# Causal masks of one more attention batch on TensorE, whole-tile copies of its scores, and a new first place in the ring of weight tiles

## The chip, the cores and the metric

One core of one Trainium2 chip. The time is in device microseconds (us) for one execution of the whole program. Engines go by the profile's names: PE is TensorE (PEld its weight loads), DVE is VectorE, ACT is ScalarE, POOL is GpSimd, SP is SyncE, which here issues the DMAs. PE, DVE and ACT each run their own list of instructions in the order in which the program has them.

## What is computed

Four batches of causal attention with a memory read-out (8 heads, 576 positions, 64 wide), then two gated layers on all 2304 tokens (512 wide, 1536 hidden):

```
scores = q k^T / 8, masked where key > query;  a = softmax(scores);  local = a v
mem    = phi(q) M_prev / (phi(q) z_prev);       x = g mem + (1 - g) local
xn     = x / rms(x) * rms_g
y      = (silu(xn w_gate) * (xn w_val)) w_out            # first layer
out    = (sigmoid(y w_gate2) * (y w_val2)) w_out2        # second layer
```

The weights come as float64.

## The kernel before

**Groups.** Tokens are worked through in five groups, numbered by `g`. Group -1 holds the first 128 positions of all four batches; groups 0 to 3 hold positions 128 to 575 (448 tokens) of one batch each, the *long* groups. For each group the main loop runs both layers (`l` = 0, 1), each over 12 slices `f` of 128 hidden units. One slice is 12 matmuls for the gate (tile `pg`), 12 for the value (`pv`), some work of ACT and DVE that makes the hidden tile `h` of them, and 12 matmuls (`po`) that add the slice's share of the output; `po` of slice f stands behind `pg` and `pv` of slice f+1. While group g is in its layers, the attention of batch g+1 is worked through in small steps (`att_steps`) between the slices, so the attention of long batch 0 lies inside group -1, and that of batch 1 inside group 0.

**Attention of a head.** `att_scores` makes transposed scores in four PSUM tiles (`ps1` to `ps4`, two buffers), with keys on the partitions. They leave PSUM for the tile `sc`; then DVE takes maxima (`mx`), POOL the maximum over partitions (`mb`), DVE subtracts it, ACT takes the exponential and writes its fp16 upper half, DVE the lower half (`pt`). `att_av` multiplies with v (`pav`), `att_mem` reads the memory (`pm`) for two heads at a time.

**The mask.** In batch 0, `st_mm` adds it inside PSUM by one more 128x128 bf16 matmul a diagonal block (`tri_b` or `tri4_b` times `ident_b`), four a head, and ACT copies each head's scores in eight pieces. In batches 1 to 3 the four diagonal blocks are written to `sc` by DVE, which adds the mask (`tri`) on the way, and the other four pieces by ACT.

**The hand-over.** After its last head, a batch is normalised (`att_norm`): ACT squares (`junk`), a row of small DVE operations for the inverse root, then for each of four tiles of 128 tokens `att_xT` has DVE scale (`xn`), ACT write the upper fp16 half and DVE the lower one (both into `x`), and SP issue a DMA transpose into `ha`. Every `pg` matmul of the next group's first slice reads columns of all four tiles, so it waits for the last transpose.

**Weights.** `slot` deals out weight tiles in a ring by the counter `ring["w"]`: in group -1 over 7 tiles (`ws`, `wl`), from group 0 on over 13, the six tiles `wr` and `wrl` being the buffers that held raw float64 weights (`raw`, `rawl`) up to then. In group 0 a gate/value pair is loaded as float32 (`both`), scaled and split into fp16 by ACT, POOL and DVE (`halve`: line 674 sums, 676 maximum, 680 upper half, 681 lower half); a slice takes three tiles there.

**Order.** The program is written step by step, and a scheduler with a model of time then sets each engine's order; `issue_after` keeps some steps behind marks of earlier slices.

Of the kernel before, what the change touches and what calls it, by code (L numbers as in the profile page):

```python
# [25 lines left out]
SO = (0, 448, 896, 1216, 1408)  # L26
SW = 1536

NEARLY = 4
NLATE = 3  # L30
# [26 lines left out]
def attn_moe_moe_kernel(ctx, tc, qT, kT, qk0, v, mz, beta, w8, rms_g, outT):  # L57
# [6 lines left out]
    nc = tc.nc  # L64
# [24 lines left out]
        out=tri, in_=tri, compare_op=ALU.is_ge, fill=NEG, base=0, pattern=[[1, 128]], channel_multiplier=-1  # L89
# [7 lines left out]
    tri_b = const.tile([128, 128], BF16, name="tri_b")  # L97
    nc.scalar.copy(out=tri_b, in_=tri)
    tri4_b = const.tile([128, 128], BF16, name="tri4_b")
# [96 lines left out]
    def softmax_weights(sc, n):  # L196
        nc.scalar.activation(out=sc[:, 0:n], in_=sc[:, 0:n], func=AF.Exp, scale=scale)  # L197
        pt = ap_.tile([128, 2, SW], F16, tag="pt", name="pt")
        nc.scalar.copy(out=pt[:, 0, 0:n], in_=sc[:, 0:n])  # L199
        nc.vector.tensor_tensor(out=pt[:, 1, 0:n], in0=sc[:, 0:n], in1=pt[:, 0, 0:n], op=ALU.subtract)  # L200
        return pt

    def st_mm(ps, c0, kq, k0, q0, n, mask=None):
        kk, qq, q2 = kq
        for i, r in enumerate((qq, q2)):
            nc.tensor.matmul(  # L206
                ps[:, c0:c0 + n], kk[:, k0:k0 + 128], r[:, q0:q0 + n], start=(i == 0), stop=(i == 1 and not mask)
            )
        if mask:
            nc.tensor.matmul(ps[:, mask[0]:mask[0] + 128], ident_b, mask[1], start=False, stop=True)  # L210
# [247 lines left out]
    def att_scores(g, h):  # L458
        kq = st.pop(("qk", g, h))
        sc = ap_.tile([128, SW], F32, tag="sc", bufs=2, name="sc")  # L460

        def diag(ps, c, kt):
            d = SO[kt]
            if g == 0:
                nc.scalar.copy(out=sc[:, d:d + 128], in_=ps[:, c:c + 128])
                return
            nc.vector.tensor_tensor(  # L467
                out=sc[:, d:d + 128], in0=ps[:, c:c + 128], in1=(tri4 if kt == 4 else tri), op=ALU.add
            )

        def cp(ps, c, d, n):
            nc.scalar.copy(out=sc[:, d:d + n], in_=ps[:, c:c + n])  # L472

        ps = late["ps"].tile([128, 512], F32, tag="pa", name="ps1")
        st_mm(ps, 0, kq, 0, 128, 448)
        cp(ps, 0, 0, 448)
        ps = late["ps"].tile([128, 512], F32, tag="pa", name="ps2")
        st_mm(ps, 0, kq, 128, 128, 448, (0, tri_b) if g == 0 else None)
        diag(ps, 0, 1)
        cp(ps, 128, SO[1] + 128, 320)  # L480
        ps = late["ps"].tile([128, 512], F32, tag="pa", name="ps3")
        st_mm(ps, 0, kq, 256, 256, 320, (0, tri_b) if g == 0 else None)
        st_mm(ps, 320, kq, 384, 384, 192, (320, tri_b) if g == 0 else None)
        diag(ps, 0, 2)
        cp(ps, 128, SO[2] + 128, 192)
        diag(ps, 320, 3)
        cp(ps, 448, SO[3] + 128, 64)
        ps = late["ps"].tile([128, 512], F32, tag="pa", name="ps4")
        st_mm(ps, 0, kq, 448, 384, 192, (64, tri4_b) if g == 0 else None)
        diag(ps, 64, 4)  # L490

        mx = ap_.tile([128, 512], F32, tag="mx", bufs=1, name="mx")
        nc.vector.tensor_tensor(out=mx[:, 0:448], in0=sc[:, 0:448], in1=sc[:, 448:896], op=ALU.max)
        for kt in (2, 3, 4):
            q = SQ[kt] - 128
            nc.vector.tensor_tensor(  # L496
                out=mx[:, q:448], in0=mx[:, q:448], in1=sc[:, SO[kt]:SO[kt] + 448 - q], op=ALU.max
            )
        mb = ap_.tile([128, 512], F32, tag="mb", bufs=1, name="mb")
        nc.gpsimd.partition_all_reduce(mb[:, 0:448], mx[:, 0:448], channels=128, reduce_op=bass_isa.ReduceOp.max)  # L500
        nc.vector.tensor_tensor(
            out=sc[:, 0:896].rearrange("p (k q) -> p k q", k=2),
            in0=sc[:, 0:896].rearrange("p (k q) -> p k q", k=2),
            in1=mb[:, None, 0:448].to_broadcast([128, 2, 448]),
            op=ALU.subtract,
        )
        for kt in (2, 3, 4):
            q, d = SQ[kt] - 128, SO[kt]
            nc.vector.tensor_tensor(  # L509
                out=sc[:, d:d + 448 - q], in0=sc[:, d:d + 448 - q], in1=mb[:, q:448], op=ALU.subtract  # L510
            )
        st["pt", g, h] = softmax_weights(sc, SW)
# [104 lines left out]
    ring = {"w": 0, "top": 0, "raw": 0}  # L617
# [46 lines left out]
    def is_half(g, l, f):  # L664
        return g >= 0 and (l == 0 or f >= NWIDE)
# [317 lines left out]
    def last_of(e):  # L983
        return next(i for i in reversed(nc.cur_bb.bb.instructions) if i.engine == e)

    def behind(pairs):

        stack = ExitStack()
        for pair in pairs:
            for i in pair:  # L990
                stack.enter_context(tc.issue_after(i))
        return stack

    for g in range(-1, B):
        n = 512 if g < 0 else S - 128
        steps = list(att_steps(g + 1)) if g + 1 < B else []

        total = 2 * NF - (6 if g < 0 else 4)

        wait = 2 if g == 0 else 1  # L1000
        done, used = 0, 0
        for l in range(2):
            early = 2 if g < 0 and l == 0 else 0
            ws, hs = early_ws[:early], early_hs[:early]
            for f in range(early):
                hidden(ws[f], l, f, 256, g, xt, hs[f], 256)
            po = None
            for f in range(NF + 1):
                if f < NF:
                    if f >= early:  # L1010
                        if g > 0 and l == 1 and f == NWIDE:
                            mid = NF if g < B - 1 else NF // 2 + 2
                            for e, c in ((nc.vector, slice(NWIDE, mid)), (nc.gpsimd, slice(mid, NF))):
                                if c.start < c.stop:
                                    e.tensor_scalar(
                                        out=unit[2][:, c],
                                        in0=unit[1][:, c],
                                        scalar1=st["half_is1"],
                                        scalar2=None,
                                        op0=ALU.mult,  # L1020
                                    )
                        with behind(marks[-2:-1] if g == 0 else []):
                            ws.append(weights(g, l, f))
                        hs.append(htiles(g, l, f))
                        hidden(ws[f], l, f, n, g, xh if l == 1 and is_half(g, l, f) else xt, hs[f])
                        marks.append(tuple(last_of(e) for e in (mybir.EngineType.Activation, mybir.EngineType.DVE)))
                if f > 0:
                    if po is None:
                        po = [late[f"po{d // 2}"].tile([128, NMAX], F32, tag=f"po{d}", name="po") for d in range(KD)]
                    out_share(ws[f - 1], hs[f - 1], po, f - 1, n)  # L1030
                    done += 1
                    with ExitStack() as after:

                        if g < 0 and done < 5:
                            traced = nc.cur_bb.bb.instructions
                            for e in (mybir.EngineType.Activation, mybir.EngineType.DVE, mybir.EngineType.SP):
                                after.enter_context(
                                    tc.issue_after(next(i for i in reversed(traced) if i.engine == e))
                                )
                        while used < len(steps) and used < len(steps) * (done - wait) // (total - wait):  # L1040
                            with behind(marks[-2:-1] if g >= 0 else []):
                                steps[used]()
                            used += 1
            if g < 0 and l == 0:
                begin.close()
            xn = wide_tokens("cd") if l == 0 else None
            for d in range(KD):
                evacuate(l, d, n, g, po[d], xn)
            if l == 0 and g >= 0:
                xh = half_tokens("b")  # L1050
                halve_tokens(n, po, xh)
            if l == 0 and g < 0:
                token_scale()
            xt = xn
        xt = st.pop("xt", None)
# [55 lines left out]
```

## Time and profile before

| | |
|---|---|
| median of 3 runs | 1062.34 us (1061.07 to 1064.21) |
| the profiled execution | 1061.58 us |
| its span, first to last instruction | 1059.8 us |
| PE busy (share of the span) | 1036.0 us (98%) |
| DVE busy | 732.3 us (69%) |
| ACT busy | 550.7 us (52%) |
| POOL busy | 90.8 us (9%) |

The span is what the views of the trace cover; 1.8 us of the execution's time lie around it. Busy shares are means over the whole span and differ much between its parts. A PE row's duration includes the pipeline's latency, so rows that follow each other overlap, and what a matmul takes of PE is read from the starts.

### The profile page before, as it was taken

What the parts mean: (1) busy time and instruction counts of PE and PEld (TensorE: products, weight loads), DVE (VectorE), ACT (ScalarE), POOL (GpSimd) and SP (SyncE); (2) the same over time, 40 slices, a digit from 0 to 9 for tenths busy, and PEclk for the clock granted to TensorE, in tenths of its full rate; (3) what the DMA queues carried; (4) which work ended last, traced back from release to release, by engine and by line L of the source; (5) the groups of instructions that cost most, each with busy time, mean ns of one, the idle gap of its engine ahead of it and who ended that gap; (6) DMA issues with size and microseconds to landing.
All of it is one profiled execution on the core that took longest, in us unless ns stands there. A gap on an engine that the chain in (4) does not pass through costs nothing.

```text
span 1059.8 us, 17506 instructions
## 1 busy us (share of the span) xinstructions
PE 1036.0 (98%) x6445; PEld 749.7 (71%) x6445; DVE 732.3 (69%) x1588; ACT 550.7 (52%) x1074; POOL 90.8 (9%) x85
## 2 busy tenths in 40 slices
PE   8899999999999989999999999999999999999998
PEld 5778887888666757676667867766777766667665
DVE  5969999898669989865677866638788654224111
ACT  4668877775568757864454543425455432112111
POOL 2301012000001101110010110000101000000000
PEclk8999999999999999999999999999999999999999
DMA  6499998884885764589754453675455437445410
GB/s 267 149 353 377 322 358 286 305 277 154 251 310 200 241 221 159 183 282 309 239 174 159 170 184 128 171 260 186 154 177 173 147 120 222 145 148 172 173 45 36
DMA packets 89686, 222.15 MB, mean 210 GB/s; under 512 B 23808, under 2 KB 29952, under 8 KB 89472
## 3 DMA queue, kind: packets, MB, share of 16 engines
q1 hardware_dynamic: 89600, 221.03, 61.7%
q8 instruction: 51, 0.84, 0.3%
q14 instruction: 35, 0.29, 0.1%
HBM read 173.28 MB, written 44.04 MB: 205 GB/s over the span
## 4 chain that ended last, share of the span: by engine, by line
PE 85%; DVE 6%; ACT 4%; DMA 2%; issue 2%; SPq 0%; ACTq 0%; DVEq 0%
PE pg L792 25%; PE po L845 25%; PE pv L792 24%; PE ps L206 4%; PE pm L565 1%; PE pav L516 1%; PE pav L518 1%; PE pav L517 1%; DMA g_bc<-in_rms_g 1%; ACT sc L197 1%; PE po L842 1%; DMA out_T<-o 1%; DMA wl<-kept 0%; DVE x L609 0%; DMA ha<-x 0%
## 5 line engine op out<-in xcount | busy, mean ns | idle before, releaser
L809 ACT ACTIVATE t<-pg,unit 128x448 f32<-128x448 f32 x88 | 55.6, 632 | 138.0 <-PE pg L792 138.0
L845 PE MATMUL po<-h,ws 128*128 128x448 f32 (+1 forms) x504 | 121.9, 384 | 0.7 <-ACT h L824 0.7
L792 PEld LDWEIGHTS <-ws 128*128 128x128 f16 x672 | 63.1, 99 | 62.6 <-issue 9.3
L845 PEld LDWEIGHTS po<-h,ws 128*128 128x128 f32 x504 | 93.8, 188 | 13.6 <-ACT h L824 0.8
L845 PE MATMUL po<-h,wl 128*128 128x448 f32 (+1 forms) x396 | 95.5, 384 | 0.0
L792 PEld LDWEIGHTS <-wr 128*128 128x128 f16 x600 | 55.8, 98 | 53.7 <-issue 5.6
L500 POOL PARTITION_ALL_REDUCE mb<-mx x32 | 59.3, 1853 | 376.9 <-DVE mx L496 360.6
L824 ACT CAST h<-t 128x448 fp32r<-128x448 f32 (+1 forms) x70 | 40.6, 581 | 87.5 <-DVE t L813 79.9
L819 DVE SCALAR_TENSOR_TENSOR t<-t,pv 128x448 f32<-128x448 f32 (+1 forms) x60 | 37.8, 630 | 68.6 <-PE pv L792 65.0
L845 PE MATMUL po<-h,wr 128*128 128x448 f32 x348 | 81.0, 377 | 0.6 <-DVE h L829 0.5
L811 DVE SCALAR_TENSOR_TENSOR t<-t,pg 128x448 f32<-128x448 f32 (+2 forms) x60 | 37.2, 619 | 64.0 <-ACT t L809 64.0
L792 PEld LDWEIGHTS <-wl 128*128 128x128 f16 x504 | 47.4, 99 | 48.1 <-issue 6.2
L845 PEld LDWEIGHTS po<-h,wl 128*128 128x128 f32 x396 | 73.8, 188 | 9.8
L845 PEld LDWEIGHTS po<-h,wr 128*128 128x128 f32 x348 | 64.9, 188 | 7.7 <-DVE h L829 0.9
L472 ACT COPY sc<-ps 128x448 f32<-128x448 f32 (+3 forms) x128 | 46.9, 372 | 42.7 <-DVE sc L467 29.7
L197 ACT ACTIVATE sc<-sc 128x1536 f32<-128x1536 f32 x32 | 47.5, 1485 | 35.2 <-DVE sc L509 35.0
L200 DVE TENSOR_TENSOR pt<-sc,pt 128x1536 f16<-128x1536 f32 x32 | 56.1, 1752 | 6.2 <-ACT pt L199 6.1
L206 PE MATMUL ps<-qq,kk 128*128 128x448 f32 (+2 forms) x160 | 55.6, 352 | 3.0 <-ACT sc L472 3.0
L825 DVE TENSOR_TENSOR h<-t,h 128x448 fp32r<-128x448 f32 (+1 forms) x70 | 46.2, 660 | 16.8 <-ACT h L824 16.3
L828 ACT ACTIVATE h<-t,unit 128x448 fp32r<-128x448 f32 x40 | 26.7, 667 | 52.3 <-DVE t L819 52.1
L792 PEld LDWEIGHTS <-wrl 128*128 128x128 f16 x336 | 31.3, 98 | 30.2 <-issue 2.5
L813 DVE SCALAR_TENSOR_TENSOR t<-t,kappa,pv 128x448 f32<-128x448 f32 x48 | 32.5, 678 | 26.1 <-PE pv L792 25.1
(259 smaller groups left out, 2474.5 us busy)
## 6 DMA issues: line engine op xcount, KB each, us to landing
raw<-in_w SPq DMA_DIRECT2D x50, 511.8 KB, 6.3
wr<-parts SPq DMA_DIRECT2D x33, 512.0 KB, 3.5
ws<-parts SPq DMA_DIRECT2D x32, 512.0 KB, 3.4
kept<-w SPq DMA_DIRECT2D x48, 256.0 KB, 5.2
wl<-parts SPq DMA_DIRECT2D x24, 512.0 KB, 3.8
ws<-half SPq DMA_DIRECT2D x23, 512.0 KB, 3.2
rawl<-in_w SPq DMA_DIRECT2D x22, 511.8 KB, 6.4
kd<-in_kT SPq DMA_DIRECT2D x64, 144.0 KB, 3.8
```

What stands on the lines that cost most here:

```text
L197: nc.scalar.activation(out=sc[:, 0:n], in_=sc[:, 0:n], func=AF.Exp, scale=scale)
L200: nc.vector.tensor_tensor(out=pt[:, 1, 0:n], in0=sc[:, 0:n], in1=pt[:, 0, 0:n], op=ALU.subtract)
L206: nc.tensor.matmul(ps[:, c0:c0 + n], kk[:, k0:k0 + 128], r[:, q0:q0 + n], start=(i == 0), stop=(i == 1 and not mask))
L472: nc.scalar.copy(out=sc[:, d:d + n], in_=ps[:, c:c + n])
L500: nc.gpsimd.partition_all_reduce(mb[:, 0:448], mx[:, 0:448], channels=128, reduce_op=bass_isa.ReduceOp.max)
L792: nc.tensor.matmul(ps[:, 0:n], w[:, a, k * 128:(k + 1) * 128], x[b][:, k, o:o + n], start=(i == 0), stop=(i == 3 * KD - 1))
L809: nc.scalar.activation(out=t, in_=pg[:, 0:n], func=AF.Tanh, scale=u[:, 0:1] if half else 0.5)
L811: nc.vector.scalar_tensor_tensor(out=t, in0=t, scalar=1.0, in1=pg[:, 0:n], op0=ALU.add, op1=ALU.mult)
L819: nc.vector.scalar_tensor_tensor(out=t, in0=t, scalar=1.0, in1=pv[:, 0:n], op0=ALU.add, op1=ALU.mult)
L824: nc.scalar.copy(out=hi, in_=t)
L825: nc.vector.tensor_tensor(out=lo, in0=t, in1=hi.bitcast(F32), op=ALU.subtract)
L845: nc.tensor.matmul(po[d][:, 0:n], w[2][:, a, c], hh[:, b, 0:n], start=(f == 0 and i == 0), stop=(f == NF - 1 and i == 2))
```

## The change

Three things. In `att_scores` the flag `by_pe` is true for batches 0 and 1 (before, batch 0 alone had the mask on PE), so batch 1's masks go from DVE to 32 more PE matmuls (4 a head, 8 heads). Where PE masks, the scores leave PSUM in four whole ACT copies of 448, 448, 512 and 128 columns, in place of eight pieces (batch 0) or of four pieces by ACT and four by DVE (batch 1). And at group 0 the ring's counter is set to 7, so that the first weight tiles of that group are those that held float64 weights, and every later tile's place in the ring moves by two.

```diff
+        by_pe = g <= 1
+
         def diag(ps, c, kt):
             d = SO[kt]
-            if g == 0:
-                nc.scalar.copy(out=sc[:, d:d + 128], in_=ps[:, c:c + 128])
-                return
             nc.vector.tensor_tensor(
                 out=sc[:, d:d + 128], in0=ps[:, c:c + 128], in1=(tri4 if kt == 4 else tri), op=ALU.add
             )
...
+        def mask(c, m):
+            return (c, m) if by_pe else None
...
-        st_mm(ps, 0, kq, 128, 128, 448, (0, tri_b) if g == 0 else None)
-        diag(ps, 0, 1)
-        cp(ps, 128, SO[1] + 128, 320)
+        st_mm(ps, 0, kq, 128, 128, 448, mask(0, tri_b))
+        if by_pe:
+            cp(ps, 0, SO[1], 448)
+        else:
+            diag(ps, 0, 1)
+            cp(ps, 128, SO[1] + 128, 320)
...
-        diag(ps, 0, 2)
-        cp(ps, 128, SO[2] + 128, 192)
-        diag(ps, 320, 3)
-        cp(ps, 448, SO[3] + 128, 64)
+        if by_pe:
+            cp(ps, 0, SO[2], 512)
+        else:
+            diag(ps, 0, 2)
+            cp(ps, 128, SO[2] + 128, 192)
+            diag(ps, 320, 3)
+            cp(ps, 448, SO[3] + 128, 64)
...
-        st_mm(ps, 0, kq, 448, 384, 192, (64, tri4_b) if g == 0 else None)
-        diag(ps, 64, 4)
+        st_mm(ps, 0, kq, 448, 384, 192, mask(64, tri4_b))
+        if by_pe:
+            cp(ps, 64, SO[4], 128)
+        else:
+            diag(ps, 64, 4)
...
         wait = 2 if g == 0 else 1
+        if g == 0:
+            ring["w"] = NEARLY + NLATE
```

The scheduler orders the engines anew. Lines of the changed kernel from `att_scores` on stand 11 further down (804 of before is 815 there), so `pv` is line 792 before and 803 now, `pm` 565 and 576.

**PE, end of group -1.** Before, at the last memory read-out of batch 0 (`pm`), which stands inside the value matmuls of slice 9:

```order
L518 MATMUL pav<-vh_119,pt 128x65
L565 MATMUL pm<-mzt,ph 128x130 x2
L792 MATMUL pv<-xc,wl 128x512
L792 MATMUL pv<-xd,wl 128x512
L792 MATMUL pv<-xc,wl 128x512
L845 MATMUL po<-h,wl 128x512 x12
L792 MATMUL pg<-xc,ws 128x512
```

Now, at the same read-out, which stands between gate and value of slice 10:

```order
L576 MATMUL pm<-mzt,ph 128x130 x2
L803 MATMUL pv<-xc,ws 128x512
L803 MATMUL pv<-xd,ws 128x512
L803 MATMUL pv<-xc,ws 128x512 x2
L803 MATMUL pv<-xd,ws 128x512
L803 MATMUL pv<-xc,ws 128x512 x2
L803 MATMUL pv<-xd,ws 128x512
L803 MATMUL pv<-xc,ws 128x512 x2
L803 MATMUL pv<-xd,ws 128x512
L803 MATMUL pv<-xc,ws 128x512
L856 MATMUL po<-h,ws 128x512 x12
L803 MATMUL pg<-xc,wl 128x512
```

Up to the first `pg` of group 0 there stood 99 more matmuls of layers behind it (3 `pv`, then `po`, `pg`, `pv`, `po`, `pg`, `pv`, `po`, `po` of 12 each); now there stand 72 (`pv`, `po`, `pg`, `pv`, `po`, `po`).

**DVE, the same end of group -1.** Before, from the end of the inverse root (587) to slice 11: scaling (604), lower halves (609), the lower half of `h` (825), products with `pv` (819; the second is slice 11's), weight splits (623):

```order
L587 SCALAR_TENSOR_TENSOR ri<-nr,ri 128x4
L604 SCALAR_TENSOR_TENSOR xn<-x,ri,g_bc 128x512 x2
L819 SCALAR_TENSOR_TENSOR t<-t,pv 128x512
L609 TENSOR_TENSOR x<-xn,x 128x512 x2
L604 SCALAR_TENSOR_TENSOR xn<-x,ri,g_bc 128x512
L825 TENSOR_TENSOR h<-t,h 128x512
L604 SCALAR_TENSOR_TENSOR xn<-x,ri,g_bc 128x512
L623 TENSOR_TENSOR wr<-w,wr 128x512
L609 TENSOR_TENSOR x<-xn,x 128x512 x2
L819 SCALAR_TENSOR_TENSOR t<-t,pv 128x512
```

Now, in part (598 is the inverse root's last, 615 scales, 620 makes lower halves, 692 is `halve`'s split, 830 is slice 11's product, 903 an output copy):

```order
L598 SCALAR_TENSOR_TENSOR ri<-nr,ri 128x4
L615 SCALAR_TENSOR_TENSOR xn<-x,ri,g_bc 128x512 x2
L692 SCALAR_TENSOR_TENSOR wr<-wr,s_3346 128x512 x2
L620 TENSOR_TENSOR x<-xn,x 128x512 x2
L830 SCALAR_TENSOR_TENSOR t<-t,pv 128x512
L615 SCALAR_TENSOR_TENSOR xn<-x,ri,g_bc 128x512 x2
L836 TENSOR_TENSOR h<-t,h 128x512
L653 TENSOR_SCALAR pw<-wtop 128x2
L634 TENSOR_TENSOR wrl<-w,wrl 128x512
L655 TENSOR_SCALAR inv<-pw 128x2
L620 TENSOR_TENSOR x<-xn,x 128x512
L903 TENSOR_SCALAR o<-po 128x512
```

All four lower halves stood ahead of slice 11's product with `pv`; now two stand behind it (the last one two rows below the piece shown, behind an output copy). The splits of group 0's first weights (692), which stood behind all of this, now stand among it.

**DVE, end of group 0.** Before, from the inverse root's last operation (829 is the lower half of `h`; the product 819 is slice 11's):

```order
L587 SCALAR_TENSOR_TENSOR ri<-nr,ri 128x4
L604 SCALAR_TENSOR_TENSOR xn<-x,ri,g_bc 128x512 x2
L829 SCALAR_TENSOR_TENSOR h<-t,unit_124,h 128x448
L609 TENSOR_TENSOR x<-xn,x 128x512 x2
L604 SCALAR_TENSOR_TENSOR xn<-x,ri,g_bc 128x512 x2
L609 TENSOR_TENSOR x<-xn,x 128x512 x2
L819 SCALAR_TENSOR_TENSOR t<-t,pv 128x448
```

Now the same stretch:

```order
L598 SCALAR_TENSOR_TENSOR ri<-nr,ri 128x4
L615 SCALAR_TENSOR_TENSOR xn<-x,ri,g_bc 128x512 x2
L830 SCALAR_TENSOR_TENSOR t<-t,pv 128x448
L620 TENSOR_TENSOR x<-xn,x 128x512 x2
L615 SCALAR_TENSOR_TENSOR xn<-x,ri,g_bc 128x512
L840 SCALAR_TENSOR_TENSOR h<-t,unit_124,h 128x448
L615 SCALAR_TENSOR_TENSOR xn<-x,ri,g_bc 128x512
L620 TENSOR_TENSOR x<-xn,x 128x512
L903 TENSOR_SCALAR o<-po 128x448
L620 TENSOR_TENSOR x<-xn,x 128x512
```

Slice 11's product moved from behind the four lower halves to ahead of them. On PE the last read-out of batch 1 stood one `pv` matmul before the end of slice 9 and now stands seven before the end of slice 10.

## Rows read from the trace of the kernel before

**Rows 1.** The page, part 1: busy us (share) xinstructions.

```profile
PE 1036.0 (98%) x6445; PEld 749.7 (71%) x6445; DVE 732.3 (69%) x1588; ACT 550.7 (52%) x1074; POOL 90.8 (9%) x85
```

**Rows 2.** Stretches: length, busy PE, PEld, DVE, ACT, POOL, granted clock, DMA, GB/s.

```profile
287.30:291.90 4.60, 4.49 (x14) 1.75 (x15) 2.83 (x4) 2.38 (x6) 0.00 (x0) 0.63 1.03 340
...
320.00:420.00 100.00, 94.57 (x658) 69.52 (x657) 92.55 (x217) 72.03 (x151) 14.07 (x15) 0.98 0.58 198
494.40:587.00 92.60, 92.59 (x595) 63.65 (x596) 64.24 (x134) 39.63 (x67) 7.03 (x5) 1.00 0.61 204
```

**Rows 3.** Chain of waits: start us, us, what; first gates of groups 1, 2.

```profile
494.41 2.43 PE pg L792 x12
...
689.22 2.43 PE pg L792 x12
```

**Rows 4.** Timeline of PE, end of group -1: start, us, line, [idle before <-releaser].

```profile
261.72 0.69 PE L565 MATMUL pm<-mzt,ph 128*128 128x130 f32 x4
...
271.18 2.96 PE L845 MATMUL po<-h,ws 128*128 128x512 f32 x12
273.98 0.40 PE L792 MATMUL pg<-xc,wl 128*128 128x512 f32 x1
...
282.40 2.89 PE L845 MATMUL po<-h,wl 128*128 128x512 f32 x12
287.35 0.55 PE L792 MATMUL pg<-ha,wl 128*128 128x448 f16 x2 [2.05 <-ACT wl L680]
```

**Rows 5.** Line 612, the transposes: windows 278 to 300, then 470 to 500.

```profile
DMA to landing us min/median/max: 3.5/4.3/5.0
...
DMA to landing us min/median/max: 2.7/3.9/4.9
```

**Rows 6.** DVE by form, 262 to 279: busy us, mean ns | idle before.

```profile
L604 DVE SCALAR_TENSOR_TENSOR xn<-x,ri,g_bc 128x512 f32<-128x512 f32 x4 | 2.9, 747 | 0.0
L609 DVE TENSOR_TENSOR x<-xn,x 128x512 f16<-128x512 f32 x4 | 2.6, 684 | 0.0
...
L586 DVE TENSOR_TENSOR nr<-nr,ss 128x4 f32<-128x4 f32 x3 | 0.5, 162 | 0.1
```

**Rows 7.** Waits of PE, 300 to 412: us in total, times, longest.

```profile
PE ps L206 <- ACT sc L472: 2.3, 2, 1.6
```

**Rows 8.** Timeline of PE in group 0, first layer.

```profile
376.92 4.11 PE L792 MATMUL pg<-ha,ws 128*128 128x448 f16 x12 [0.46 <-DVE t L811]
```

**Rows 9.** Timeline of PE: scores with a mask (batch 0), without (batch 1).

```profile
105.19 0.23 PE L210 MATMUL ps<-tri_b,ident_b 128*128 128x128 bf16 x1
105.23 0.34 PE L206 MATMUL ps<-qq,kk 128*128 128x192 f32 x1
...
105.52 0.23 PE L210 MATMUL ps<-tri_b,ident_b 128*128 128x128 bf16 x1
...
338.73 0.25 PE L206 MATMUL ps<-qq,kk 128*128 128x192 f32 x1
...
338.93 0.28 PE L206 MATMUL ps<-qq,kk 128*128 128x192 f32 x1
```

**Rows 10.** Line 467, DVE's masks: ns min/median/max, first and last start.

```profile
L467 DVE TENSOR_TENSOR sc<-ps,tri x96: 273/284/294, 317.7 to 851.4; 128x128 f32<-128x128 f32 x96
```

**Rows 11.** ACT by form, 300 to 480: copies of scores.

```profile
L472 ACT COPY sc<-ps 128x448 f32<-128x448 f32 x8 | 4.2, 524 | 5.8 <-PE ps L206 5.8
L472 ACT COPY sc<-ps 128x320 f32<-128x320 f32 x8 | 3.3, 414 | 1.4 <-DVE sc L467 1.4
```

**Rows 12.** Waits of PE, 158 to 176, group -1: us in total, times, longest.

```profile
PE pg L792 <- ACT t L809: 1.1, 1, 1.1
```

**Rows 13.** Timeline of PE, end of group 0.

```profile
477.84 2.44 PE L792 MATMUL pg<-hb,wr 128*128 128x448 f16 x12
...
484.83 2.44 PE L792 MATMUL pg<-hb,wr 128*128 128x448 f16 x12
...
491.79 2.60 PE L845 MATMUL po<-h,wrl 128*128 128x448 f32 x12
```

More of the change, by code (lines that the diff above doesn't have):

```diff
@@ L477, in att_scores @@
         ps = late["ps"].tile([128, 512], F32, tag="pa", name="ps2")
-        st_mm(ps, 0, kq, 128, 128, 448, (0, tri_b) if g == 0 else None)
-        diag(ps, 0, 1)
-        cp(ps, 128, SO[1] + 128, 320)
-        ps = late["ps"].tile([128, 512], F32, tag="pa", name="ps3")
-        st_mm(ps, 0, kq, 256, 256, 320, (0, tri_b) if g == 0 else None)
-        st_mm(ps, 320, kq, 384, 384, 192, (320, tri_b) if g == 0 else None)
-        diag(ps, 0, 2)
-        cp(ps, 128, SO[2] + 128, 192)
-        diag(ps, 320, 3)
-        cp(ps, 448, SO[3] + 128, 64)
-        ps = late["ps"].tile([128, 512], F32, tag="pa", name="ps4")
-        st_mm(ps, 0, kq, 448, 384, 192, (64, tri4_b) if g == 0 else None)
-        diag(ps, 64, 4)
+        st_mm(ps, 0, kq, 128, 128, 448, mask(0, tri_b))
[4 more added lines that the diff above has]
+            cp(ps, 128, SO[1] + 128, 320)
+        ps = late["ps"].tile([128, 512], F32, tag="pa", name="ps3")
+        st_mm(ps, 0, kq, 256, 256, 320, mask(0, tri_b))
+        st_mm(ps, 320, kq, 384, 384, 192, mask(320, tri_b))
+        if by_pe:
[5 more added lines that the diff above has]
+            cp(ps, 448, SO[3] + 128, 64)
+        ps = late["ps"].tile([128, 512], F32, tag="pa", name="ps4")
+        st_mm(ps, 0, kq, 448, 384, 192, mask(64, tri4_b))
[3 more added lines that the diff above has]
+            diag(ps, 64, 4)
         mx = ap_.tile([128, 512], F32, tag="mx", bufs=1, name="mx")
```

## The prediction

> **What bounds the kernel now.** I read the page's busy shares first: PE is busy 98% of the span [rows 1], so what the change moves matters only where PE stands still, runs at its lower clock, or gets more to do. So next the starts of each group's first gate. Group 0 starts at 287.35 [rows 4], group 1 at 494.41 and group 2 at 689.22 [rows 3]: group 0 takes 207.1 us and group 1 takes 194.8, with the same matmuls. These 12.3 us are what a change to group 0 can win there. The stretches say what they are: from 320 to 420 PE has 5.4 us idle while DVE is busy 92.6 of 100, whereas group 1's first layer has PE without a gap and DVE at 64 of 92.6 [rows 2]. PE's waits in that part of group 0 are short and of many kinds, the largest for scores that leave PSUM [rows 7]. After one of them twelve gates took 4.11 us [rows 8] where they otherwise take 2.43 [rows 3]: the granted clock had dropped to its half, and that costs 1.7 us each time. One more such place is the hand-over from group -1 to 0: the last `po` ends at 285.29, PE stands 2.05 us for the upper half of the first weights (line 680) [rows 4], and the next 4.6 us have a mean clock of 0.63 [rows 2].
>
> **The masks on PE.** With a mask, a block of scores of 192 columns takes 0.33 us from one mask matmul's start to the next (105.19 to 105.52); without, 0.20 (338.73 to 338.93) [rows 9]. The mask's own slot is only 0.04 us (105.19 to 105.23), the rest is the weight load of the next matmul, which so short a matmul doesn't cover. So 0.13 us, times 32 in group 0: **+4.2 us**, all of it on PE, the engine that bounds. Bounds: 32 x 0.04 = 1.3 (if all the loads hide) and 32 x 0.23, the whole duration of a mask row, = 7.4. The Trainium skill, in "TensorE: Matmul & The Clock Gate", section "Back-to-back issue gap", gives about 81 ns per matmul of 128 columns in a stream of loads and matmuls. By that the masks would cost 2.6 us and the sum would end 1.6 us lower. The rows here are above it, since the neighbours of these masks are float32r with longer loads, and I go by the rows.
>
> **What DVE and ACT get.** DVE loses 32 masks of 0.28 us [rows 10], 9 us at most, most of it where it is near full. ACT's count of copies in batch 1 stays at four a head but 512 columns more go through them; 128 columns cost 0.11 us (524 against 414 ns) [rows 11], so 0.44 us a head, 3.5 us in all, under cover of an ACT that is busy 72 of 100 us [rows 2]; without that cover it would stand on the path of the scores, +3.5. In batch 0 ACT saves four copies a head; PE has next to nothing to gain from that in group -1, save one wait of 1.1 us for a `tanh` [rows 12] behind an exponential, which stands ahead of that exponential in the new order: **-1.1** (bounds -1.8, with a smaller wait for scores beside it, and 0). In group 0 the scores no longer pass between DVE and ACT in turns. Of the 7.1 us (5.4 idle, 1.7 of half clock) I take two thirds as gone: **-5**. The bounds are 0 (DVE is still some 86 of 100, and other waits are behind the first) and 12.3 less the half clock at the group's start, -10.5.
>
> **Weight tiles.** The first weights of group 0 now load while slices 10 and 11 of group -1 run, and ACT's work on them lies ahead of the `po` that end it. So the wait of 2.05 us for line 680 goes. What is late next is the input, `ha`.
>
> **Hand-over to group 0.** The new order has batch 0's last read-out (`pm`) later: 72 matmuls stand behind it in place of 99. Twelve take 2.80 us (271.18 to 273.98) [rows 4], so PE reaches the first gate 6 x 2.8 = 16.8 us after it; before it was 285.29 less 262.41 = 22.9. In that time the normalisation must finish, and its last pieces are in DVE's queue behind other work. From slice 10's product with `pv` (which cannot start before that `pv` ends, 2.8 + 0.3 for the latency = 3.1 us) to the last lower half, DVE's list has 17 instructions of 512 columns and 18 of a few columns. The long ones take 0.65 us each in a row (2.6 us for four of line 609, a little more for 604), the short ones 0.2 (0.162 and a third of the 0.1 idle before three of them) [rows 6]: 17 x 0.65 + 18 x 0.2 = 14.6, ending at 17.7 without any wait. The last transpose is issued then and lands 3.5 us later at the soonest of this hand-over [rows 5], at 21.2. PE waits 4.4 us as a floor, and I take 4.8, with some waiting on ACT and POOL in that chain; in place of 2.05 that is **+2.8** (bounds +1.5 with a landing of 2.7, the shortest seen, and +4). The half clock after it is there before and after. Nothing else can run: all of group 0 stands behind this gate in PE's list.
>
> **Hand-over to group 1.** The same happens at the end of group 0. Before, the gates start at 494.41 [rows 3], 2.62 us after the last twelve `po` started [rows 13]: no gap. Now `pm` has behind it 7 `pv` (1.3 us), `po` (2.4), the whole of a slice (477.84 to 484.83, 7.0) and the last `po` (2.6) [rows 13]: 13.3 us. Slice 11's `pv` ends at 8.2. Its product on DVE, from 8.5 on, has behind it eight long instructions up to the last lower half, where before all lower halves were ahead of it: 9 x 0.63 = 5.7, so 14.2; with a landing of 2.7 to 3.9 [rows 5] `ha` is there at 16.9 to 18.1. PE waits 3.6 to 4.8 us where it waited for nothing: **+4.2**. Such a gap was followed by half clock above, so **+1.7** more. Later hand-overs keep their order.
>
> **The sum:** 4.2 - 1.1 - 5 + 2.8 + 4.2 + 1.7 = +6.8. The profiled execution took 1061.58 us, so 1068.4. The median of the three runs is 0.8 above that execution, so against it the same working gives 1069; I say 1068.5.
>
> **Rivals.**
> 1. *Both inputs arrive in time* (ends on the other side). For it: before, they did at all hand-overs. Against: the counts above. It decides at one point, whether the last transpose lands before the last `po` ends, for which DVE's stretch would have to be over 4 us shorter in both places. Then the old gap and its half clock go too: 4.2 - 1.1 - 5 - 2.05 - 1.7 = -5.7, so 1056; with all of group 0's loss gone, 1050.
> 2. *DVE still bounds group 0.* The stalls there only change their names: for it, DVE's 92.6 of 100 loses no more than a tenth, and the 5.4 us were of many kinds. Then +11.8, 1073.4.
> 3. *No change.* Group 0 loses all of its stalls (-10.5) and the hand-overs cost their floors (2.3 and 3.6): 4.2 - 1.1 - 10.5 + 2.3 + 3.6 + 1.7 = +0.2, so 1061.8. For it: with DVE at 64 of 92.6, group 1 has no stall at all.
>
> **Chances.** The forecast 0.5, rival 1 0.09, rival 2 0.2, rival 3 0.21. A measurement here tells about 0.3% (3.2 us) from no change. Faster by more than that (under 1059.2) is rival 1, with a little of rival 3: 0.1. Within it (up to 1065.5): rival 3 and the forecast's lower end, 0.24. Slower: 0.66. The forecast's own range is 1064 to 1072; for 8 in 10 it reaches over rivals 2 and 3: 1058 to 1075.
>
> **What would show it.** Right: at both hand-overs PE's first gate waits 3 to 6 us for `ha` from the DMA, each followed by a mean clock near 0.6; the wait for line 680 is gone; 32 mask matmuls in group 0 with 0.3 us from mask to mask within a tile; DVE's line of masks at 64; PE idle from 320 to 420 under 3 us. Wrong: gates that start with the end of the last `po` at either hand-over (rival 1), or idle of 5 us and more in group 0's first layer (rival 2), or under 1 us there (rival 3). I am wrong also if the new places of tiles in the ring make weights late in groups 1 to 3, which the sum has at nothing: there the pairs are loaded several slices ahead, and a late one would cost a PE wait of a microsecond or two each.

## The result, and the profile after

The changed kernel takes 1067.26 us (median of 5 runs, 1065.77 to 1069.02) where the kernel before takes 1062.34: a ratio of 1.0052, interval 1.0039 to 1.0064. It is slower by half a per cent, 1.2 us less than forecast. The profiled execution took 1067.58 us, 6.0 more than that of before; the working had +6.8.

The page of the changed kernel, part 1, answers to [rows 1]: PE has 32 instructions more, DVE 32 fewer, and PE's share falls by a point, since the span has grown by more than PE's work.

```profile
PE 1038.0 (97%) x6477; PEld 750.9 (70%) x6477; DVE 728.9 (68%) x1556; ACT 552.5 (52%) x1042; POOL 90.1 (8%) x85
```

PE's timeline at the first gates of groups 0, 1 and 2 (start, us, line, idle before it and what ended it):

```profile
289.02 3.81 PE L803 MATMUL pg<-ha,wr 128*128 128x448 f16 x12 [4.20 <-DMA ha<-x]
...
497.69 4.63 PE L803 MATMUL pg<-ha,ws 128*128 128x448 f16 x12 [6.96 <-DMA ha<-x]
...
695.38 2.43 PE L803 MATMUL pg<-ha,wrl 128*128 128x448 f16 x12 [0.26 <-DMA ha<-x]
```

The reader is to see two things: what stands in the brackets, and the time of twelve gates behind it. At groups 0 and 1 PE now waits for the input, 4.20 and 6.96 us; before it was 2.05 for weights [rows 4] and nothing [rows 3, 13]. Twelve gates take 2.43 us at full clock and 4.63 behind the longer wait. The stretches say the same (columns as in [rows 2]): the start of group 0, its first layer, the gap ahead of group 1, and the start of group 1.

```profile
289.00:293.60 4.60, 4.58 (x17) 2.07 (x18) 0.76 (x2) 1.23 (x2) 0.00 (x0) 0.69 0.97 290
320.00:420.00 100.00, 98.86 (x673) 72.34 (x672) 88.63 (x196) 77.57 (x161) 13.28 (x15) 1.00 0.63 216
...
490.70:497.70 7.00, 0.04 (x2) 0.04 (x2) 0.65 (x1) 0.54 (x1) 0.00 (x0) 0.68 1.10 222
...
497.70:502.30 4.60, 4.60 (x13) 1.86 (x14) 0.62 (x1) 0.00 (x0) 0.00 (x0) 0.50 0.92 273
```

From 320 to 420 PE's idle time fell from 5.4 to 1.1 us, and DVE from 92.6 to 88.6 of 100. PE's waits from 300 to 412 were of five kinds, the largest of them in [rows 7]; one is left:

```profile
PE pav L529 <- DVE pt L200: 1.0, 1, 1.0
```

So the change does in group 0 what it says, and pays for it at two gates. The chain of waits ahead of group 1's gate (start, us, what) shows which work the gate waited for:

```profile
484.39 1.24 DVE xn L615 x2
485.73 0.62 DVE t L830
486.34 1.20 DVE x L620 x2
487.54 0.66 DVE xn L615
488.21 0.61 DVE h L840
...
490.65 0.70 DVE x L620
491.36 1.33 SPq L623
492.78 4.78 DMA ha<-x
497.69 4.63 PE pg L803 x12
```

It is read from below: the gate waits for a transpose under way for 4.78 us; this one stood on SP's queue (SPq) behind the transpose ahead of it; and that behind the normalisation on DVE, among which slice 11's product (830) and hidden tile (840) stand.

### The profile page after: what moved, and what is told of

It reads as the page before. It is cut to its first block, busy times and chain, and to the rows that moved or that the text cites. A ratio compares the mean times of both kernels' runs of the same rounds, so it can differ in the third digit from the quotient of the medians.

```text
span 1065.8 us, 17489 instructions
## 1 busy us (share of the span) xinstructions
PE 1038.0 (97%) x6477; PEld 750.9 (70%) x6477; DVE 728.9 (68%) x1556; ACT 552.5 (52%) x1042; POOL 90.1 (8%) x85
## 4 chain that ended last, share of the span: by engine, by line
PE 87%; ACT 3%; DVE 2%; DMA 2%; issue 1%; SPq 0%; ACTq 0%; POOL 0%; DVEq 0%; POOLq 0%
PE pg L803 26%; PE po L856 26%; PE pv L803 25%; PE ps L206 4%; PE pm L576 1%; PE pav L527 1%; PE pav L529 1%; PE pav L528 1%; DMA ha<-x 1%; PE po L853 1%; DMA ws<-parts 1%; PE ps L210 0%; ACT t L820 0%; ACT pt L199 0%; ACT vh L169 0%
## 5 line engine op out<-in xcount | busy, mean ns | idle before, releaser
L856 PE MATMUL po<-h,ws 128*128 128x448 f32 (+1 forms) x480 | 117.3, 385 | 0.2
L803 PEld LDWEIGHTS <-wr 128*128 128x128 f16 x624 | 58.4, 99 | 60.2 <-issue 6.3
L856 PEld LDWEIGHTS po<-h,ws 128*128 128x128 f32 x480 | 89.1, 188 | 13.1 <-ACT h L835 0.5
L856 PE MATMUL po<-h,wr 128*128 128x448 f32 x372 | 85.9, 376 | 0.0
L856 PEld LDWEIGHTS po<-h,wr 128*128 128x128 f32 x372 | 69.8, 188 | 6.8
L471 ACT COPY sc<-ps 128x448 f32<-128x448 f32 (+5 forms) x128 | 52.4, 421 | 41.3 <-DVE sc L466 23.0
L206 PE MATMUL ps<-q,kk 128*128 128x448 f32 (+2 forms) x160 | 49.4, 318 | 0.0
```

The costliest lines, as they stand in the source:

```text
L206: nc.tensor.matmul(ps[:, c0:c0 + n], kk[:, k0:k0 + 128], r[:, q0:q0 + n], start=(i == 0), stop=(i == 1 and not mask))
L803: nc.tensor.matmul(ps[:, 0:n], w[:, a, k * 128:(k + 1) * 128], x[b][:, k, o:o + n], start=(i == 0), stop=(i == 3 * KD - 1))
L856: nc.tensor.matmul(po[d][:, 0:n], w[2][:, a, c], hh[:, b, 0:n], start=(f == 0 and i == 0), stop=(f == NF - 1 and i == 2))
```

## The terms, measured

| term | forecast | measured | from |
|---|---|---|---|
| 32 masks on PE | +4.2 | +3.3 | starts on PE in group 0: 21 masks stand ahead of a float32r matmul and take 0.04 us, and that matmul 0.085 more; 11 stand ahead of a 16-bit one and take 0.055 to 0.067 |
| `tanh` wait, group -1 | -1.1 | -0.9 | this wait: 1.1 before, 0.2 now (the group as a whole ended 0.5 sooner, 284.82 for 285.29) |
| group 0's stalls | -5 | -8.4 | the remainder: group 0 without its gap went from 207.06 to 201.71 (-5.35), and the masks (+3.3) and the half clock at its start (-0.3) are taken out |
| hand-over to group 0 | +2.8 | +2.15 | 4.20 for 2.05 |
| half clock behind it | 0 | -0.3 | 4.6 us at 0.63 before [rows 2], at 0.69 now |
| hand-over to group 1 | +4.2 | +7.0 | 6.96 for 0 |
| half clock behind it | +1.7 | +2.9 | group 1 from gate to gate: 194.81 before, 197.69 now |
| sum | +6.8 | +5.8 | the spans differ by 6.0; the third row is a remainder, so this agreement doesn't test it |

## The experiments

The theory, A: the change is slower because `ha` is late at two gates, and what makes it late is where the batch's last read-out (`pm`) stands in PE's list and what DVE then does ahead of the last lower half. Rivals: the weight tiles (B), stalls that only move (C), masks or copies as such (D). The ratios are to the kernel before, run on the same chip. A cut diff is against the kernel that its sentence names, and `...` marks what is left out of it.

**One part at a time.** The ring alone:

```diff
+        if g == 0:
+            ring["w"] = NEARLY + NLATE
```

> The kernel before with the ring's counter set to 7 at group 0 and nothing else of the change. Theory A (the time lost lies at the two gates that wait for the input ha, and what makes ha late is where the last read-out stands: 72 and 67 layer matmuls behind it in the changed kernel): here 91 stand behind it at the hand-over to group 0 and 103 at the one to group 1, so there is no wait of 3 us and more for ha at either; the wait of 2.05 us for line 680 is gone, what is left there is 0 to 1.5 us; group 0's own stalls stay. About 1060.5 us, 1059 to 1062.5. Rival B (the new places of the weight tiles cost the time): weight loads appear among the waits of PE in groups 0 to 3, and the time is 1064 or more.

1060.50 us, ratio 0.998 (0.997 to 0.9991). At group 0 there is no wait at all, at group 1 0.74 us for `ha`; no wait for weights appears among PE's larger ones. B falls: by itself the ring gives 0.2%.

Batch 0's whole copies alone (the diff is against the changed kernel):

```diff
-        by_pe = g <= 1
+        by_pe = g <= 0
...
-        if g == 0:
-            ring["w"] = NEARLY + NLATE
```

> Batch 0's scores in four whole copies, the rest as before (batch 1 masked by DVE, ring as before). Theory A: the four copies alone move batch 0's last read-out from 99 to 72 matmuls before the gate of group 0, so that gate waits some 4.2 us for ha from the DMA (2.05 for weights before); the wait of 1.1 us for tanh in group -1 is gone; group 0's stalls stay (5 us idle); 133 matmuls behind the read-out of batch 1, so no wait at group 1. About 1063, 1061.5 to 1064.5. Rival B (the wait for ha at group 0 comes from the weight splits that the new ring puts among the last lower halves on DVE): that gate starts within 2.5 us of the last po and the time is about 1061.

1065.64 us, ratio 1.0023 (1.0007 to 1.0039), with a wide spread (1062.07 to 1068.87). My expectation of the place was wrong: the gate waits 0.63 us, not 4, though 72 matmuls stand behind the read-out. At group 1 I had expected no wait, and there was one (both rows):

```profile
287.28 0.54 PE L803 MATMUL pg<-ha,wl 128*128 128x448 f16 x2 [0.63 <-ACT kappa L699]
...
494.45 2.43 PE L803 MATMUL pg<-ha,wrl 128*128 128x448 f16 x12 [1.04 <-DMA ha<-x]
```

So the read-out's place is not enough at group 0; the rival that I put beside it was right about the gate. The last lower half ends 15.4 us behind the read-out here, and 17.5 in the changed kernel. DVE's rows of the changed kernel show what lies between:

```profile
276.86 1.41 DVE L692 SCALAR_TENSOR_TENSOR wr<-wr,s 128x512 f16<-128x512 f32 x2
...
283.95 0.69 DVE L903 TENSOR_SCALAR o<-po 128x512 f32<-128x512 f32 x1
...
284.63 0.67 DVE L620 TENSOR_TENSOR x<-xn,x 128x512 f16<-128x512 f32 x1
```

The two weight splits that the new ring puts there (692) and the output copy (903), which stands behind the last lower half in the run with the copies alone, take 1.41 and 0.69, which covers the 2.0 us of difference. The profiled execution was among the fastest of its twelve, so that the median's 3.5 us more aren't explained by this trace.

Batch 1's masks and copies alone; batch 0 keeps its eight pieces, the ring its place (against the changed kernel, in part):

```diff
+        whole = g == 1
...
-        if by_pe:
+        if whole:
```

> Batch 1 masked by PE and copied whole, batch 0 in eight pieces and the ring as before. Theory A: 99 matmuls behind batch 0's read-out, so the hand-over to group 0 is as before (2.05 us for line 680); 67 behind batch 1's, so group 1's first gate waits about 7 us for ha, followed by half clock (2.9 us); group 0's stalls are gone (-5.9) and 32 masks cost about 1.5 (0.045 each): +5.5, about 1068. By a mask price of 0.13 us (the prediction's) 1070.5. Rival B (the gap at group 1 comes from the ring or from batch 0): no gap there, about 1058.

1067.92 us, ratio 1.0054 (1.0035 to 1.0073): the whole loss comes back with this part alone, as A expected, and at the place it named.

```profile
496.50 4.64 PE L807 MATMUL pg<-ha,wrl 128*128 128x448 f16 x12 [6.93 <-DMA ha<-x]
```

The change without the ring:

> The change without the ring's new place. Theory A'': the 4.2 us at group 0 need both the later read-out and the weight splits that the new ring puts among DVE's last lower halves. So the gate of group 0 starts within 1 us of the last po, as with batch 0's copies alone, and the half clock behind it goes; the 7 us at group 1 and the half clock there stay, and so do the gone stalls: 1067.3 - 3.6 - 1.4 = about 1062.3, 1060.5 to 1064. Rival (the read-out's place alone makes that wait): 4 us at group 0, 1067.

1065.06 us, ratio 1.003 (1.0019 to 1.0041); 2.8 above what I expected. The wait of 4.2 us at group 0 did go, but 1.74 us of PE waiting for `h` from ACT took its place just ahead (with half clock behind it), and the gap at group 1 was 8.28 us, 1.3 more than in the changed kernel. So in the whole change the ring costs some 2 us, where alone it gains as much.

**Lateness by itself.** The kernel before with batch 1's attention one slice later, and nothing of the change:

```diff
-        total = 2 * NF - (6 if g < 0 else 4)
+        total = 2 * NF - (6 if g < 0 else (3 if g == 0 else 4))
```

> The kernel before, with nothing of the change, and group 0's attention one slice later, so that 69 layer matmuls stand behind batch 1's last read-out in place of 97 (67 in the changed kernel). Theory A: lateness alone makes the gap at group 1: 3 to 4.5 us of waiting for ha, less than the 7 of the changed kernel since one lower half fewer stands behind slice 11's product, and 1.4 to 2.8 of half clock behind it; group 0's stalls stay or shrink a little: about 1067, 1064 to 1069. Rival D (the gap needs the masks on PE or the whole copies): no wait for ha over 1 us at group 1, 1062.

1068.16 us, ratio 1.0063 (1.0048 to 1.0078).

```profile
497.87 4.63 PE L792 MATMUL pg<-ha,wrl 128*128 128x448 f16 x12 [4.55 <-DMA ha<-x]
```

The gap of 4.55 us and the half clock come with no mask moved and no copy changed. D falls.

A stronger dose, the kernel before with the ring and total 18:

```diff
-        total = 2 * NF - (6 if g < 0 else 4)
+        total = 2 * NF - (6 if g <= 0 else 4)
...
+        if g == 0:
+            ring["w"] = NEARLY + NLATE
```

> The kernel before with the new ring and total 18 in place of 20 at group 0, no mask moved and batch 0 in eight pieces. The scheduler then puts batch 1's last read-out not earlier but later: 42 layer matmuls stand behind it (6 pg, 12 pv, 24 po: 1.2 + 2.4 + 5.2 = 8.8 us), against 97 in the kernel before and 67 in the changed one. Theory A as a dose: the chain from the read-out to the landing takes about 19 us whatever stands on PE (20.4 in the changed kernel, here with one product of a slice fewer on DVE), so the gate of group 1 waits some 10 us for ha, 9 to 12, and 2.3 to 2.8 of half clock follow: about 1072.5 us, 12 above the run with the ring alone; 1070 to 1075. Rival (a wait at a gate is bounded by something that is full at the time, so that 7 us is about its limit): 1069 or less.

1067.14 us, ratio 1.0037 (1.0023 to 1.0052). The gap is the one worked out:

```profile
497.79 4.66 PE L792 MATMUL pg<-ha,ws 128*128 128x448 f16 x12 [10.27 <-DMA ha<-x]
```

The time isn't: 5.4 us less than expected, in the rival's range, though a gap of 10 us rules out the rival's limit of about 7. Group 0 up to its gap took 205.4 us here (282.16 to 497.79, less 10.27) against 209.0 with the ring alone, so attention in this order stalls PE less, and my sum had taken the stalls as they were. The place of the last read-out over several kernels (for the kernel before and the changed one it is read from these rows: the last number of the first and last start):

```profile
L565 PE MATMUL pm<-mzt,ph x8: 274/275/357, 468.6 to 475.1; 128*128 128x130 f32 x8
```

```profile
L576 PE MATMUL pm<-mzt,ph x8: 274/275/358, 471.7 to 477.0; 128*128 128x130 f32 x8
```

| kernel | layer matmuls behind batch 1's last read-out | read-out | first gate of group 1 | between, us | wait for `ha` |
|---|---|---|---|---|---|
| changed, attention one slice earlier (below) | 156 | 461.6 | 492.08 | 30.5 | 0 |
| batch 0's copies alone | 133 | 467.0 | 494.45 | 27.5 | 1.04 |
| attention ends two slices earlier (below) | 129 | 463.3 | 488.48 | 25.2 | 0 |
| ring alone | 103 | 471.8 | 492.91 | 21.1 | 0.74 |
| before | 97 | 475.1 | 494.41 | 19.3 | 0 |
| before, attention later | 69 | 479.1 | 497.87 | 18.8 | 4.55 |
| changed | 67 | 477.0 | 497.69 | 20.7 | 6.96 |
| batch 1's masks alone | 67 | 475.4 | 496.50 | 21.1 | 6.93 |
| changed without the ring | 67 | 473.3 | 495.37 | 22.1 | 8.28 |
| ring, total 18 | 42 | 479.0 | 497.79 | 18.8 | 10.27 |

Where the gate waited, `between` is the chain from read-out to input. With 42 to 103 matmuls behind the read-out it takes 19 to 22 us, and PE is done first. It isn't a constant, though, and the count alone doesn't decide: with batch 0's copies alone it took 27.5 us, so that the gate waited although 133 matmuls stood behind. There the last lower half ended 19.7 us behind the read-out (14.4 in the changed kernel), and its transpose landed 7.7 later. In the kernel before the last transpose landed at 494.28, 0.13 us ahead of its gate: it had no slack that a change could use.

**The last transposes.** The changed kernel with the last of batch 1's four transposes issued by ACT:

```diff
-        nc.sync.dma_start_transpose(
+        q = nc.scalar if g == 1 and t == 3 else nc.sync
+        q.dma_start_transpose(
```

> The whole change, with the last of batch 1's four transposes issued by ACT in place of SP. Theory A': of the 6.2 us between the last lower half and the landing of its transpose, about 1.5 are SP's, busy with an output store and the third transpose; then the wait at group 1 falls from 7.0 to about 5.5 and the time to about 1065.8. Rival (the landing is set by the DMA engines, busy with weights and the other transposes): the wait stays at 6.5 to 7, 1067.3.

1070.22 us, ratio 1.0074 (1.0058 to 1.009): worse by 3, and the wait is 8.83 us. The end of the chain of waits ahead of that gate, and ACT's waits (the row gives count, times and first and last start):

```profile
496.49 2.63 DMA ha<-x
499.12 0.14 issue
499.26 0.90 PE pg L804 x2
...
L624 ACTq EVENT_SEMAPHORE  x2: 38/38/38, 496.3 to 496.4; - x2
```

The transpose on ACT's queue stands behind two instructions (EVENT_SEMAPHORE) that wait for the semaphores of SP's transposes. They ran at 496.33 and 496.41, right after SP's last transpose had landed (496.31). (The chain names an output store of SP as the releaser; that store landed at 496.77, after the issue, and its semaphore isn't among those waited for.) The Trainium skill, "DMA: Bandwidth & Descriptors", section "Silent corruption: two transposing streams in flight at once", says that the first transpose of a later stream must wait for the full completion of the earlier one; the trace agrees with such a wait, 0.2 us from landing to issue. So this run couldn't take the two transposes apart, as I had meant. It shows that the last transpose, issued then, lands after 2.63 us (4.78 in the changed kernel). The third one (490.72 to 496.31) took 5.6 with no transpose behind it, but it moves 128 tokens, and the last one only 64 (448 is three times 128 and 64).

The changed kernel without the stores of group 0's outputs:

> The whole change, with the four stores of group 0's outputs left out (that part of the output is not written). Theory A' (the two last transposes before group 1's gate are slow because output stores share SP's queue and the DMA engines with them): issue 0.4 us sooner and landing 4.5 in place of 4.8 to 5.9, so the wait for ha falls from 7.0 to 5.5 or less and the time to about 1065.5. Rival (weight loads and the transposes themselves fill the DMA engines): the wait stays within 0.5 us of 7.0 less the 0.4, about 1067.

1067.99 us, ratio 1.0054 (1.004 to 1.0067). The last landing took 3.78 us in place of 4.78, the wait 6.08 in place of 6.96; between the two expectations. The transpose wasn't issued sooner (1.56 us behind its lower half, 1.43 in the changed kernel). In these two executions the stores make 0.9 of the 7 us, all of it in the landing, and the time doesn't show it.

**The masks' price, and attention that ends earlier.** The changed kernel with group 0's attention one slice earlier:

```diff
-        wait = 2 if g == 0 else 1
+        wait = 1
```

> The whole change, with group 0's attention spread over its slices one slice earlier (wait is 1 at group 0 as in the other groups, in place of 2), so that 156 matmuls stand behind batch 1's last read-out in place of 67. Theory A: the wait of 7 us for ha at group 1 and the 2.9 us of half clock behind it go, and the 4.2 us at group 0 stay: about 1057.5, 1056 to 1059.5, 0.45% below the kernel before. Rival C (attention that is pressed into fewer slices brings DVE's stalls of group 0 back, some 5 us): about 1062.5.

1062.22 us, ratio 1.0006 (0.9994 to 1.0017). The gate of group 1 starts at 492.08 without a wait, as A says, but 5 us are back, not 9.8, which is the time that C had. PE's timeline shows where a part of the rest is, in group 0's early slices:

```profile
334.32 1.86 PE L803 MATMUL pg<-ha,ws 128*128 128x448 f16 x9 [1.44 <-DVE t L822]
```

With a wait of 1.3 us for DVE between the layers and one of 0.7 for `ha` at group 2, less the 1.0 that is gone, that is 2.4 us of new waits; another 1.4 is a longer half clock behind the wait at group 0. So C is right for a quarter of what the gate gave back, and some 1 us stays open.

The same with batch 0 in eight pieces, which takes away the gap at group 0 too:

> Batch 1 masked by PE and copied whole, the new ring, group 0's attention one slice earlier; batch 0 stays in eight pieces. Theory A: neither gate waits for ha (91 layer matmuls behind batch 0's last read-out, 156 behind batch 1's). Against the changed kernel that takes away 4.2 us and 1.4 of half clock at group 0 and 7.0 and 2.8 at group 1; the tanh wait of group -1 comes back (+1.1), and waits of some 2.5 us as in the run with attention one slice earlier: about 1055.5 us, 1053.5 to 1058. Rival C (what these gates give back turns up as stalls of group 0, all of it): 1062, as with attention one slice earlier.

1058.94 us, ratio 0.9967 (0.9953 to 0.998), 3.4 above what I expected and outside my range. Neither gate waits for `ha`; the wait for DVE in the early slices has grown to 2.67:

```profile
330.48 2.43 PE L807 MATMUL pg<-ha,ws 128*128 128x448 f16 x12 [2.67 <-DVE t L826]
```

So I kept the beginning and moved only the end (wait 2, and total 18 at group 0 as in the run of the dose):

> As the run before it with batch 1's masks and the ring (batch 0 in eight pieces), but group 0's attention begins where it did (wait is 2) and ends two slices earlier (total 18 in place of 20): 129 layer matmuls behind batch 1's last read-out. Theory A: no wait for ha at either gate, and the wait of 2.7 us for DVE in group 0's second and third slices, which came with beginning one slice earlier, is gone: about 1056.3 us, 1054.5 to 1058.5. Rival C (attention in fewer slices makes stalls wherever it begins): 1059 or more.

1058.60 us, ratio 0.997 (0.9959 to 0.9982): faster than both kernels, by 0.3% and 0.8%. But it is 2.3 above what I expected and no better than its neighbour: the wait for DVE went, and 2.0 us for ACT's `h` between the layers and 1.4 for a weight half came (C again).

```profile
PE po L860 <- ACT h L839: 2.0, 1, 2.0
PE pg L807 <- ACT ws L695: 1.4, 1, 1.4
```

Three masks for one in batch 1, in that kernel:

> The same kernel with every mask matmul of batch 1 made three times (96 in place of 32; the mask is added three times, which changes no weight that is not masked away). By the slots of the changed kernel's trace (48 ns from a mask's start to the next matmul's) 64 more cost 3.1 us; by the prediction's 0.13 us they cost 8.3. So 3.1 above its pair, about 1059.5, against 1064.5.

1062.94 us, 4.3 above its pair by the medians and 2.4 by the profiled spans: nearer to 3.1 than to 8.3. The pair differs in more than the masks, since the scheduler put batch 1's last read-out 143 matmuls ahead of the gate in place of 129. Three masks in a row take 0.15 us of PE:

```profile
346.15 0.34 PE L212 MATMUL ps<-tri_b,ident_b 128*128 128x128 bf16 x3
346.30 1.05 PE L862 MATMUL po<-h,wl 128*128 128x448 f32 x4
```

That is 0.05 a mask. A 192-column block takes 0.17 us behind three masks as behind one, so what is added to the next matmul is paid once, and this run doesn't price it.

## Why the prediction was right, and where it was off

**The masks.** The price of 0.13 us holds for the case from which it was read. A mask takes 0.04 us, and the float32r matmul behind it takes 0.085 more than otherwise, whatever its width: 0.17 for 0.09 with 192 columns, 0.29 for 0.20 with 448.

```profile
323.98 0.23 PE L210 MATMUL ps<-tri_b,ident_b 128*128 128x128 bf16 x1
324.02 0.34 PE L206 MATMUL ps<-qq,kk 128*128 128x192 f32 x1
324.19 0.27 PE L206 MATMUL ps<-q,kk 128*128 128x192 f32 x1
...
393.72 0.23 PE L210 MATMUL ps<-tri_b,ident_b 128*128 128x128 bf16 x1
393.76 0.45 PE L803 MATMUL pg<-xc,wr 128*128 128x448 f32 x1
394.05 0.36 PE L803 MATMUL pg<-xd,wr 128*128 128x448 f32 x1
394.25 0.57 PE L803 MATMUL pg<-xc,wr 128*128 128x448 f32 x2
```

But 11 of the 32 stand ahead of a 16-bit matmul (317.04 below), which takes no longer, and cost some 0.066; so the mean is 0.10.

```profile
317.04 0.22 PE L210 MATMUL ps<-tri_b,ident_b 128*128 128x128 bf16 x1
317.10 0.73 PE L803 MATMUL pg<-ha,wr 128*128 128x448 f16 x3
```

**Group 0's stalls.** The mechanism held and the size didn't: -8.4 for -5. "Two thirds as gone" was too few: of the 5.4 us idle 4.3 went, and the 1.7 of half clock too, so 6.0 of the 7.1 that I counted. The other 2.4 of this remainder are not among the waits that I counted. Waits that are shorter than a matmul's row, and so show only in the starts, don't explain them: from the starts (each matmul's time to the next start, held against the median of its kind between the same neighbours) I estimate 1.4 us of such waits in group 0 before and 1.2 now. The matmuls also stand in another order, with other neighbours; what the 2.4 us are stays open. The bound of -10.5 held. Rival 2 fell. Rival 3's condition (all stalls gone) came near: 1.1 us idle, and its sign was under 1. What kept the time above rival 3 was mostly the gate of group 1 (3.6 us there, 6.96 measured) and the half clock behind it.

**Hand-over to group 0.** Right in the count: DVE was to end 17.7 us after the read-out and ended 17.5 after it; the floor was 4.4 and the wait 4.20. The rest is partly luck: SP's queue, which the working had left out here too, took 0.7 us between the last lower half and the issue, and the landing took 3.0 where 3.5 was taken.

**Hand-over to group 1.** The counts were right: `po` ends 13.8 us behind the read-out (13.3 forecast), the last lower half 14.4 (14.2). The step that failed is the next one, "with a landing of 2.7 to 3.9 [rows 5] `ha` is there at 16.9 to 18.1": it was there at 20.6. From the end of the last lower half it took 6.2 us. Of these 1.4 are SP's queue: the third transpose was ready at 490.07, but a weight load and an output store were ahead of it, and the fourth had to wait for its issue:

```profile
489.82 0.83 SPq L769 DMA_DIRECT2D wr<-parts  x1
490.75 0.37 SPq L911 DMA_DIRECT2D out_T<-o  x1
491.17 3.23 SPq L623 DMA_TRANSPOSE ha<-x  x2
```

The other 4.8 are the landing, near the longest of [rows 5] and not its median. I had counted every instruction of DVE and none of SP. What made this landing longer than the 2.71 us of before is shown only in part: 1.0 went with the output stores left out.

**Half clock.** That it would follow at group 1 was right. Its +1.7 was taken from twelve gates behind a short wait inside group 0 (4.11 us for 2.43 [rows 8]), and here it cost 2.9. Its length doesn't follow from the wait's alone (last section).

The misses, 3.4 us too little gained in group 0 and 4.0 too little paid at group 1 (2.8 of waiting, 1.2 of half clock), nearly cancel. That the sum is better than its terms is luck. Rival 1 fell at both gates, and no weight was late in groups 1 to 3.

## What to carry to other kernels

Where one stage hands over to the next, count from the last step that feeds the hand-over: what its chain takes (here mostly 19 to 22 us, transposes and their queue included) against the work that the bounding engine has left behind it. A change that makes a stage smoother can put that step later in a scheduler's order and lose more at the gate than it won; look at the order of the hand-over first, and give the step an earlier place together with the change. Count the issue queue of the transfers like an engine, and take the landing time from a place that is as busy.

## What the runs showed of the hardware

The granted clock behind an idle PE did not follow the length of the wait alone. Twelve gates take 2.43 us at the full 2.4 GHz. They took 4.66 after 4.32 us in one kernel (changed, attention one slice earlier), but 3.79 after 8.28 us in another (changed without the ring):

```profile
287.62 4.66 PE L803 MATMUL pg<-ha,wr 128*128 128x448 f16 x12 [4.32 <-DMA ha<-x]
...
495.37 3.79 PE L803 MATMUL pg<-ha,wrl 128*128 128x448 f16 x12 [8.28 <-DMA ha<-x]
```

After 6.96 and 10.27 us they took 4.63 and 4.66 (clock 0.50), after 4.20 us 3.81, and 2.05 us before were followed by a mean of 0.63 [rows 2]. Inside group 0, in the run with batch 1's masks, the ring and attention one slice earlier, they took 2.43 after 2.67 us (clock 1.00), while in the kernel before they took 4.11 after 0.46 us [rows 8], with 1.59 us of idle 0.9 us ahead of it. What PE had done before those waits differs, and which of it decides stays open.

In the hand-overs to groups 0 and 1 of all these kernels a transpose occupied its queue for 1.2 to 3.9 us and landed 2.6 to 7.8 us after its issue. The shortest landings (2.6 to 2.7) are those of fourth transposes, which move 64 tokens. The longest is a third one, in the run with batch 0's copies alone.
